# Retention followed by a routed feed-forward layer on one core: input loads, weight loads and two batches' feed-forward work moved between loop turns

## The chip, the cores and the metric

The kernel runs on one core of a Trainium2 chip. The metric is the device time of one execution in microseconds. Before the change three runs gave a median of 123.45 us (122.86 to 124.14). A core has five engines with a queue of instructions each: PE (matrix multiply; its weight loads are listed as PEld), DVE (VectorE), ACT (ScalarE), POOL (GpSimd) and SP, which here only issues transfers. Every engine works through its own queue in order and waits for others through semaphores. The transfers run on 16 DMA engines that SP's and POOL's issues share.

## The reference

Shapes: q, k, v are (4 batches, 8 heads, 768 positions, 64). The second layer has w_gate (512), w1 (512 x 1024), w2 (1024 x 512) and a capacity of 128.

```python
gamma = 1.0 - 2.0 ** (-5.0 - np.arange(H))
for t in range(S):                       # retention: a decaying state per head
    state = gamma * state + einsum('bhd,bhe->bhde', k[:, :, t], v[:, :, t])
    y[:, :, t] = scale * einsum('bhd,bhde->bhe', q[:, :, t], state)
x = y.transpose(0, 2, 1, 3).reshape(B, S, H * D)

scores = einsum('bsd,d->bs', x, w_gate)  # routing: 128 of 768 tokens of a batch
for b in range(B):
    top_idx = argpartition(-scores[b], capacity)[:capacity]
    xe = x[b, top_idx]
    ye = np.maximum(xe @ w1, 0.0) @ w2
    g = 1.0 / (1.0 + np.exp(-scores[b, top_idx]))
    out[b, top_idx] = x[b, top_idx] + g[:, None] * ye    # out is x elsewhere
```

## The kernel before, in words

The 768 positions of a batch are cut into three blocks of 256, so there are 12 blocks, numbered m = 0 to 11; block m belongs to batch b = m // 3 and is its block r = m % 3. The recurrence is written in chunks of 128: matmuls inside a chunk under a causal mask, and a state that is carried from chunk to chunk. All matmuls are bf16.

**The way of one block.**

- `load(m)` (L57) issues five transfers on SP: two halves of q, two of k, one of v, together 1.57 MB. The tiles lie in a pool of five buffers for each of q, k and v.
- `cast(m)` (L179) runs on POOL: qb is q times a decay table, kc is k in bf16, vb is v times a table. Four buffers of each.
- `transposes(m, "q")` and `(m, "k")` (L191) on PE, each copied out of PSUM by ACT as qT and kT. `turn_back(m)` (L201) transposes kT back to kb.
- `scores(m, part)` (L211): matmuls into pa, and a masking multiply on DVE into am.
- `inside(m)`, `across(m, u, py)` and `update(m, u)`: the outputs py of two chunks, and the state matmuls pst with their copies S on ACT.
- `finish(m, py)` (L270): ACT copies py to the output tile xo, DVE sums the routing scores from py (its product goes to a tile called junk). `put(m, xo)` (L284) issues two output stores on SP, 0.52 MB together.

**The way of one batch through the second layer.**

- `route_spread` and `route_beats` run once for each block: the scores are transposed to a row (pr) and compared (DVE, L315, L319, L322). `route_ranks` (PE, pk) and `route_index` (DVE, L354 and L357, idx) run once the three blocks of a batch are there.
- `route_fetch` (L360) is an indirect transfer on POOL's queue that gathers the 128 chosen rows from the output in memory into xg. It needs the batch's output stores to have landed, and the index.
- `route_gate` (product with w_gate: POOL for batches 0 to 2, DVE for batch 3), `route_turn` (PE transposes pg, copied by ACT as xT), `route_sigmoid` (ACT sums and takes exp, DVE adds one and takes the reciprocal).
- `ffn_up(b, 0)` and `(b, 1)` (matmuls ph, relu copy hT on ACT), `ffn_down` (matmuls pd), `ffn_add` (DVE, ye), `route_put` (indirect store on POOL's queue).

pr, pk, pg, ph, pd and the pb of `turn_back` take turns in one PSUM pool, psM, of two buffers, in the order of the program.

**The weights.** `load_weights(part)` (L159) is called for four parts: two halves of w1, two halves of w2. Each is a transfer on POOL's queue that reads 1.05 MB in f32 and writes 0.52 MB in bf16.

**The order.** The program is written in the order in which each engine is to work. Ahead of the loop stand `load(0)` to `load(3)` and the casts of blocks 0 and 1. The loop (L472) has 12 passes, here called turns. Turn m does, in this order: `load(m + 4)`; place -1; `cast(m + 2)`; in turns 1 to 4 one part of the weights; the q transposes of block m + 1; the second half of block m's scores; an update; place 0; the k transposes of block m + 1; place 1; `inside`, `across`, `finish`, an update, `put`; place 2; the first half of block m + 1's scores and `turn_back(m + 1)`; places 3 and 4. The routing and feed-forward steps are put into these places by a table (L441 to L458), entered as `at(turn, place, step)`; several steps at one place run in the order in which they were entered, which is by the last block of their batch. With m the last block of batch b (2, 5, 8, 11), the steps of a batch hang on the turn d of its fetch:

```python
            d = m + 3 if b < B - 2 else m + 2
            at(d, -1, route_fetch, b)
            at(d + 2, -1, route_gate, b)
            at(d + 2, 2, route_turn, b)
            at(d + 2, 4, route_sigmoid, b)
            at(d + 3, 0, ffn_up, b, 0)
            at(d + 3, 2, ffn_up, b, 1)
            at(d + 3, 3, ffn_down, b)
            at(d + 4, 1, ffn_add, b)
            at(d + 5, -1, route_put, b)
```

So d is 5, 8, 10, 13. What falls on turn 12 or later runs behind the loop, in the order of turns and places: the routing of batch 3 from its last block on, and all that is left of the feed-forward work.

Of the kernel before, what the change touches and what calls it, by code (L numbers as in the profile page):

```python
# [9 lines left out]
FT = mybir.dt.float32  # L10
BF = mybir.dt.bfloat16
# [7 lines left out]
def kernel(ctx: ExitStack, tc: tile.TileContext, q, k, v, w_gate, w1, w2, capacity, out):  # L19
    nc = tc.nc  # L20
    B, H, S, D = q.shape
    C = 128
# [3 lines left out]
    Dm = H * D  # L26
# [4 lines left out]
    NBLK = B * NM  # L31
# [11 lines left out]
    store = ctx.enter_context(tc.tile_pool(name="store", bufs=4))  # L43
    perb = ctx.enter_context(tc.tile_pool(name="perb", bufs=2))
# [12 lines left out]
    def load(m):  # L57
        b, r = divmod(m, NM)
        for nm, src in (("q", q), ("k", k), ("v", v)):
            ap = src[b, :, r * T:(r + 1) * T, :]  # L60
            if nm != "v":
                t = loads.tile([128, 2, 8, D], FT, name=nm + "f", tag=nm + "f")
                for half in range(2):
                    nc.sync.dma_start(t[:, half].rearrange("p j d -> p (j d)"),
                                      bass.AP(tensor=ap.tensor, offset=ap.offset + half * S * D,
                                              ap=[[8 * D, T // 8], [2 * S * D, HP], [1, 8 * D]]))
            else:
                t = loads.tile([128, H, 2, D], FT, name=nm + "f", tag=nm + "f")
                ap = bass.AP(tensor=ap.tensor, offset=ap.offset, ap=[[2 * D, 128], ap.ap[0], [1, 2 * D]])
                nc.sync.dma_start(t.rearrange("p h j d -> p h (j d)"), ap)  # L70
            raw[nm, m] = t
# [65 lines left out]

    load(2)
    load(3)
    before = consts.tile([128, C], FT)  # L140
    tokrow = consts.tile([128, S], FT)
    slotcol = consts.tile([128, 1], FT)
# [16 lines left out]
    def load_weights(part):  # L159
        if part < 2:  # L160
            n = DD // 2
            nc.gpsimd.dma_start(w1s[:, part * n:(part + 1) * n, :],
                                bass.AP(tensor=w1.tensor, offset=w1.offset + part * n * 128 * F,
                                        ap=[[F, 128], [128 * F, n], [1, F]]))
        else:
            n = FB // 2
            part -= 2
            nc.gpsimd.dma_start(w2s[:, part * n:(part + 1) * n, :],
                                bass.AP(tensor=w2.tensor, offset=w2.offset + part * n * 128 * Dm,
                                        ap=[[Dm, 128], [128 * Dm, n], [1, Dm]]))  # L170
# [8 lines left out]
    def cast(m):  # L179
        r = m % NM  # L180
        kc = nats.tile([128, 8, 2, D], BF, name="kc", tag="kc")
        vb = nats.tile([128, 2, H, D], BF, name="vb", tag="vb")
        qb = nats.tile([128, 8, 2, D], BF, name="qb", tag="qb")
        nc.gpsimd.tensor_mul(qb, raw["q", m].rearrange("p h j d -> p j h d"),  # L184
                             gq[:, r, :, :, None].to_broadcast([128, 8, 2, D]))
        nc.gpsimd.tensor_copy(kc, raw["k", m].rearrange("p h j d -> p j h d"))  # L186
        nc.gpsimd.tensor_mul(vb, raw["v", m].rearrange("p h j d -> p j h d"),  # L187
                             gv[:, 2 * r:2 * r + 2, :, None].to_broadcast([128, 2, H, D]))
        nat[m] = (kc, vb, qb)

    def transposes(m, nm):  # L191
        src = nat[m][2 if nm == "q" else 0]
        pt = psT.tile([128, 8, T // 8, HP], BF, name="pt", tag="pt")
        for i in range(8):
            nc.tensor.transpose(pt[:, i].rearrange("p s g -> p (s g)"), src[:, i], ident)  # L195
        t = work.tile([128, HP, T], BF, name=nm + "T", tag=nm + "T")
        nc.scalar.activation(t.rearrange("p g (s i) -> p g s i", i=8), pt.rearrange("p i s g -> p g s i"), AF.Copy)  # L197
        tr[nm, m] = t
# [12 lines left out]
    def scores(m, part):  # L211
        qT, kT = tr["q", m], tr["k", m]
        pa = psA.tile([128, 2, 2, 2, C], FT, name="pa", tag="pa")
        for d in range(2):
            dd = 2 * part + d
            for j in range(2):
                for u in range(2):
                    for half in range(2):
                        r = slice(half * 64, half * 64 + 64)
                        nc.tensor.matmul(pa[u * 64:u * 64 + 64, half, d, j, :], kT[r, dd, u * C:(u + 1) * C].rearrange("p (s j) -> p s j", j=2)[:, :, j],  # L220
                                         qT[r, dd, u * C:(u + 1) * C], start=True, stop=True)
        am = work.tile([128, 2, 2, 2, C], BF, name="am", tag=f"am{part}")
        nc.vector.tensor_mul(am.rearrange("p a b c d -> p (a b) (c d)"), pa.rearrange("p a b c d -> p (a b) (c d)"),  # L223
                             causal.rearrange("p a b -> p (a b)")[:, None, :].to_broadcast([128, 4, 2 * C]))
        att[m, part] = am
# [3 lines left out]
    def inside(m):  # L229
        vb = nat[m][1]  # L230
        py = [psY.tile([C, H, D], FT, name=f"py{u}", tag=f"py{u}") for u in range(2)]
        for h in range(H):
            dd, half = divmod(h, 2)
            for j in range(2):
                for u in range(2):
                    r = slice(u * 64, u * 64 + 64)
                    nc.tensor.matmul(py[u][:, h, :], att[m, dd // 2][r, half, dd % 2, j, :], vb[r, j, h, :],  # L237
                                     start=(h == 0 and j == 0), stop=True, skip_group_check=True)
        return py
# [30 lines left out]
    def finish(m, py):  # L270
        b, r = divmod(m, NM)
        if r == 0:
            batch[b] = {"sc": perb.tile([128, NC], FT, name="sc", tag="sc")}
        xo = store.tile([C, 2, Dm], FT, name="xo", tag="xo")

        for u in range(2):
            nc.scalar.activation(xo[:, u, :], py[u].opt(), AF.Copy)  # L277
            w = 1 - u
            junk = store.tile([C, Dm], BF, name="junk", tag="junk")
            nc.vector.scalar_tensor_tensor(junk, py[w].opt(), 1.0, wgB, OP.mult, OP.mult,  # L280
                                           accum_out=batch[b]["sc"][:, 2 * r + w:2 * r + w + 1])
        return xo
# [76 lines left out]

    def route_fetch(b):  # L360
        st = batch[b]
        xg = perb.tile([128, Dm], FT, name="xg", tag="xg")
        nc.gpsimd.indirect_dma_start(  # L363
            out=xg, out_offset=None, in_=flat[:(b + 1) * S], in_offset=bass.IndirectOffsetOnAxis(ap=st["idx"][:, 0:1], axis=0),
            bounds_check=(b + 1) * S - 1, oob_is_err=True)
        st["xg"] = xg
# [71 lines left out]
    def at(t, place, f, *args):  # L438
        slots.setdefault((t, place), []).append((f, args))

    for m in range(NBLK):  # L441
        b, r = divmod(m, NM)
        at(m + 1, 0, route_spread, b, r)
        at(m + 1, 1, route_beats, b, r)
        if r == NM - 1:
            at(m + 1, 3, route_ranks, b)
            at(m + 1, 4, route_index, b)

            d = m + 3 if b < B - 2 else m + 2
            at(d, -1, route_fetch, b)  # L450
            at(d + 2, -1, route_gate, b)
            at(d + 2, 2, route_turn, b)
            at(d + 2, 4, route_sigmoid, b)
            at(d + 3, 0, ffn_up, b, 0)
            at(d + 3, 2, ffn_up, b, 1)
            at(d + 3, 3, ffn_down, b)
            at(d + 4, 1, ffn_add, b)
            at(d + 5, -1, route_put, b)  # L458

    def slot_work(t, place):  # L460
        for f, args in slots.pop((t, place), ()):
            f(*args)
# [7 lines left out]
    turn_back(0)  # L470

    for m in range(NBLK):  # L472
        if m + 4 < NBLK:
            load(m + 4)
        slot_work(m, -1)
        if m + 2 < NBLK:
            cast(m + 2)
        if 1 <= m < 5:
            load_weights(m - 1)
        if m + 1 < NBLK:  # L480
            transposes(m + 1, "q")
        scores(m, 1)
        update(m, 0)
        slot_work(m, 0)
        if m + 1 < NBLK:
            transposes(m + 1, "k")
        slot_work(m, 1)
        py = inside(m)
        for u in range(2):
            across(m, u, py)  # L490
        xo = finish(m, py)
        update(m, 1)
        put(m, xo)
        slot_work(m, 2)
        if m + 1 < NBLK:
            scores(m + 1, 0)
            turn_back(m + 1)
        slot_work(m, 3)
        slot_work(m, 4)
# [37 lines left out]
```

## Time and profile before

| | us |
|---|---|
| median of three runs | 123.45 (122.86 to 124.14) |
| the profiled execution | 123.08 |
| its span in the trace | 121.4 |
| PE busy | 83.1 (68%) |
| DVE busy | 75.0 (62%) |
| ACT busy | 76.8 (63%) |
| POOL busy | 77.2 (64%) |

Transfers: 29.88 MB, mean 246 GB/s over the span; 25.43 MB of them on SP's queue, 4.20 MB on POOL's (counted by what is written). No engine is busy over the whole span, so the page is read by stretches of time. On the timelines a line gives the start, the duration, the engine, the source line, the operation with its output and inputs, and, in brackets, how long the engine had stood idle before it and what ended that. All times count from the start of the span. PE's pipelined matmuls are merged into one line for a group.

### The profile page before, as it was taken

What the parts mean: (1) busy time and instruction counts of PE and PEld (TensorE: products, weight loads), DVE (VectorE), ACT (ScalarE), POOL (GpSimd) and SP (SyncE); (2) the same over time, 40 slices, a digit from 0 to 9 for tenths busy, and PEclk for the clock granted to TensorE, in tenths of its full rate; (3) what the DMA queues carried; (4) which work ended last, traced back from release to release, by engine and by line L of the source; (5) the groups of instructions that cost most, each with busy time, mean ns of one, the idle gap of its engine ahead of it and who ended that gap; (6) DMA issues with size and microseconds to landing.
All of it is one profiled execution on the core that took longest, in us unless ns stands there. A gap on an engine that the chain in (4) does not pass through costs nothing. (4 is left out here: it accounts for less than half of the span.)

```text
span 121.4 us, 4113 instructions
## 1 busy us (share of the span) xinstructions
PE 83.1 (68%) x1701; PEld 64.9 (53%) x1708; DVE 75.0 (62%) x217; ACT 76.8 (63%) x141; POOL 77.2 (64%) x72
## 2 busy tenths in 40 slices
PE   0046798968676896609959879796497785694920
PEld 0034576856664685408847768474495663371700
DVE  6001347689899788913987849489759394924120
ACT  6233587999976699905578999593489942431500
POOL 6658999999998290899659999799034000231230
PEclk9999999999999999965799999999769999999998
DMA  2999999999999999999999999985215113203202
GB/s 58 299 299 343 337 343 364 345 346 391 296 280 275 344 279 290 370 365 283 327 389 360 387 359 392 354 297 192 92 24 195 48 57 115 86 5 86 86 0 86
DMA packets 25250, 29.88 MB, mean 246 GB/s; under 512 B 1552, under 2 KB 14864, under 8 KB 25232
## 3 DMA queue, kind: packets, MB, share of 16 engines
q1 hardware_dynamic: 22992, 25.43, 62.6%
q0 software_dynamic: 2240, 4.20, 14.7%
q8 instruction: 13, 0.21, 0.7%
q14 instruction: 5, 0.04, 0.1%
HBM read 24.38 MB, written 7.34 MB: 261 GB/s over the span
## 5 line engine op out<-in xcount | busy, mean ns | idle before, releaser
L223 DVE TENSOR_TENSOR am<-pa,causal 128x1024 bf16<-128x1024 f32 x24 | 29.3, 1222 | 21.2 <-PE pa L220 21.1
L187 POOL TENSOR_TENSOR vb<-vf,gv 128x1024 bf16<-128x1024 f32 x12 | 22.8, 1900 | 6.1 <-DMA vf<-in_v_dram 6.1
L184 POOL TENSOR_TENSOR qb<-qf,gq 128x1024 bf16<-128x1024 f32 x12 | 22.8, 1904 | 4.9 <-DMA qf<-in_q_dram 4.8
L197 ACT ACTIVATE qT<-pt 128x1024 bf16<-128x1024 bf16 x12 | 12.3, 1022 | 14.3 <-PE pt L195 14.3
L277 ACT ACTIVATE xo<-py 128x512 f32<-128x512 f32 x24 | 14.4, 600 | 8.0 <-DVE junk L280 6.5
L195 PE MATMUL pt<-ident,qb 128*128 128x128 bf16 x96 | 9.5, 257 | 12.0 <-POOL qb L184 12.0
L280 DVE SCALAR_TENSOR_TENSOR junk<-py,wgB 128x512 bf16<-128x512 f32 x24 | 15.6, 689 | 1.8 <-PE py L247 1.8
L268 ACT ACTIVATE S<-pst 64x256 bf16<-64x256 f32 x40 | 14.9, 373 | 1.0 <-PE pst L263 0.4
L220 PE MATMUL pa<-qT,kT 64*64 64x128 bf16 x384 | 11.7, 243 | 5.6 <-DVE am L223 4.0
L431 POOL DMA_INDIRECT out_dram<-ye,idx x4 | 4.2, 1040 | 16.9 <-DVE ye L426 13.6
L195 PEld LDWEIGHTS <-qb 128*128 128x128 bf16 x96 | 7.4, 116 | 13.0 <-POOL qb L184 12.7
L197 ACT ACTIVATE kT<-pt 128x1024 bf16<-128x1024 bf16 x12 | 12.3, 1021 | 2.1 <-PE pt L195 2.1
L186 POOL CAST kc<-kf 128x1024 bf16<-128x1024 f32 x12 | 12.4, 1036 | 1.6 <-DMA kf<-in_k_dram 1.6
L208 ACT ACTIVATE kb<-pb 128x1024 bf16<-128x1024 bf16 x12 | 12.3, 1022 | 1.8 <-PE pb L206 1.7
L220 PEld LDWEIGHTS <-kT 64*64 64x64 bf16 x384 | 7.9, 118 | 8.1 <-issue 4.6
L263 PE MATMUL pst<-vb,kb 64*64 64x64 bf16 x320 | 9.5, 203 | 1.6 <-ACT kb L208 1.6
L195 PE MATMUL pt<-ident,kc 128*128 128x128 bf16 x96 | 8.8, 244 | 2.0 <-ACT qT L197 1.6
L341 PE MATMUL pk<-beats,ones 128*128 128x512 bf16 (+3 forms) x29 | 5.8, 304 | 6.0 <-ACT kb L208 4.5
L237 PE MATMUL py<-vb,am 64*128 64x64 bf16 x384 | 9.0, 198 | 1.0 <-issue 0.6
L195 PEld LDWEIGHTS <-kc 128*128 128x128 bf16 x96 | 7.6, 111 | 3.6 <-issue 2.5
L263 PEld LDWEIGHTS <-kb 64*64 64x64 bf16 x320 | 7.8, 118 | 3.2 <-ACT kb L208 2.3
L363 POOL DMA_INDIRECT xg<-out_dram,idx x4 | 4.3, 1084 | 8.1 <-PE pa L220 3.8
(79 smaller groups left out, 147.6 us busy)
## 6 DMA issues: line engine op xcount, KB each, us to landing
qf<-in_q_dram SPq DMA_DIRECT2D x24, 256.0 KB, 6.5
kf<-in_k_dram SPq DMA_DIRECT2D x24, 256.0 KB, 7.1
vf<-in_v_dram SPq DMA_DIRECT2D x12, 512.0 KB, 9.7
out_dram<-xo SPq DMA_DIRECT2D x24, 256.0 KB, 6.1
w1s<-in_moe_w_dram POOLq DMA_DIRECT2D x2, 512.0 KB, 8.6
w2s<-in_moe_w_dram POOLq DMA_DIRECT2D x2, 512.0 KB, 10.3
wgB<-in_moe_w_gate_dram SPq DMA_DIRECT2D x1, 256.0 KB
xg<-out_dram,idx POOLq DMA_INDIRECT x4, 5.2
```

The lines of the kernel that those rows point to most:

```text
L184: nc.gpsimd.tensor_mul(qb, raw["q", m].rearrange("p h j d -> p j h d"), gq[:, r, :, :, None].to_broadcast([128, 8, 2, D]))
L186: nc.gpsimd.tensor_copy(kc, raw["k", m].rearrange("p h j d -> p j h d"))
L187: nc.gpsimd.tensor_mul(vb, raw["v", m].rearrange("p h j d -> p j h d"), gv[:, 2 * r:2 * r + 2, :, None].to_broadcast([128, 2, H, D]))
L195: nc.tensor.transpose(pt[:, i].rearrange("p s g -> p (s g)"), src[:, i], ident)
L197: nc.scalar.activation(t.rearrange("p g (s i) -> p g s i", i=8), pt.rearrange("p i s g -> p g s i"), AF.Copy)
L208: nc.scalar.activation(kb.rearrange("p j h d -> p (j h d)"), pb.rearrange("p j g x -> p (j g x)"), AF.Copy)
L220: nc.tensor.matmul(pa[u * 64:u * 64 + 64, half, d, j, :], kT[r, dd, u * C:(u + 1) * C].rearrange("p (s j) -> p s j", j=2)[:, :, j], qT[r, ...
L223: nc.vector.tensor_mul(am.rearrange("p a b c d -> p (a b) (c d)"), pa.rearrange("p a b c d -> p (a b) (c d)"), causal.rearrange("p a b -> ...
L263: nc.tensor.matmul(pstate[b][half * 64:half * 64 + 64, dd, :], kb[r, j, h, :], vb[r, j, h, :], start=(c == 0 and dd == 0 and j == 0), stop ...
L268: nc.scalar.activation(t[r, :, half * 64:half * 64 + 64], pstate[b][r], AF.Copy)
L277: nc.scalar.activation(xo[:, u, :], py[u].opt(), AF.Copy)
L280: nc.vector.scalar_tensor_tensor(junk, py[w].opt(), 1.0, wgB, OP.mult, OP.mult, accum_out=batch[b]["sc"][:, 2 * r + w:2 * r + w + 1])
```

## The change

`load(4)` joins the loads ahead of the loop, and turn m issues `load(m + 5)` instead of `load(m + 4)`; the pool of five buffers is as it was. The four weight parts are issued in turns 2, 4, 6 and 7 instead of 1, 2, 3 and 4. The fetches of batches 0 and 1 go one turn later (d is 6, 9, 10, 13), and all that hangs on them with them. `ffn_down` goes from place 3 to place 4 for every batch. The output tile xo has six buffers instead of four, junk two instead of four, the gathered tile xg three instead of two.

With these turns the table meets itself in two turns: batch 0's up and down matmuls fall on turn 9, where batch 2's ranks are made; batch 1's fall on turn 12, behind the loop, beside the routing of batch 3. Batch 1's sigmoid falls on turn 11, place 4, so that its gate steps on DVE stand ahead of the last beats, where before batch 1's add stood.

```diff
@@ -137,6 +137,7 @@
     load(2)
     load(3)
+    load(4)
@@ -271,12 +272,12 @@
-        xo = store.tile([C, 2, Dm], FT, name="xo", tag="xo")
+        xo = store.tile([C, 2, Dm], FT, name="xo", tag="xo", bufs=6)
...
-            junk = store.tile([C, Dm], BF, name="junk", tag="junk")
+            junk = store.tile([C, Dm], BF, name="junk", tag="junk", bufs=2)
@@ -359,7 +360,7 @@
-        xg = perb.tile([128, Dm], FT, name="xg", tag="xg")
+        xg = perb.tile([128, Dm], FT, name="xg", tag="xg", bufs=3)
@@ -446,14 +447,14 @@
-            d = m + 3 if b < B - 2 else m + 2
+            d = m + (4, 4, 2, 2)[b]
...
-            at(d + 3, 3, ffn_down, b)
+            at(d + 3, 4, ffn_down, b)
@@ -470,13 +471,13 @@
-        if m + 4 < NBLK:
-            load(m + 4)
+        if m + 5 < NBLK:
+            load(m + 5)
         slot_work(m, -1)
         if m + 2 < NBLK:
             cast(m + 2)
-        if 1 <= m < 5:
-            load_weights(m - 1)
+        if m in (2, 4, 6, 7):
+            load_weights((2, 4, 6, 7).index(m))
```

## The prediction

> **What bounds the kernel now.** I read the 40 slices first, then sums over stretches, then the timelines of POOL, PE, ScalarE and DVE where a stretch looked odd. Slices of 3.03 us:
>
> ```profile
> POOL 6658999999998290899659999799034000231230
> PEclk9999999999999999965799999999769999999998
> DMA  2999999999999999999999999985215113203202
> ```
>
> Transfers run without a gap until about 80 us, then hardly at all. PEclk dips twice, in slices 17-19 (52-61 us) and 28-29 (85-91 us). The stretches (PE, PEld, DVE, ACT, POOL busy, clock, DMA share, GB/s) say which engine starves:
>
> ```profile
> 30.00:40.00 10.00, 6.58 (x163) 5.25 (x163) 9.29 (x26) 7.83 (x13) 9.49 (x8) 1.00 1.11 288
> 40.00:50.00 10.00, 8.47 (x240) 6.86 (x237) 8.47 (x23) 8.96 (x16) 4.37 (x4) 1.00 1.11 316
> 50.00:60.00 10.00, 5.82 (x134) 4.93 (x126) 5.52 (x17) 4.94 (x8) 9.16 (x7) 0.66 1.12 328
> ```
>
> From 40 to 50 POOL, the first station of every block, works only 4.37 of 10 us; from 50 to 60 PE, DVE and ACT starve. POOL's timeline tells why:
>
> ```profile
> 42.73 1.89 POOL L184 TENSOR_TENSOR qb<-qf,gq 128x1024 bf16<-128x1024 f32 x1 [2.51 <-DMA qf<-in_q_dram]
> 48.74 1.90 POOL L187 TENSOR_TENSOR vb<-vf,gv 128x1024 bf16<-128x1024 f32 x1 [3.13 <-DMA vf<-in_v_dram]
> 50.58 0.80 POOL L168 DMA_DIRECT2D w2s<-in_moe_w_dram  x1
> 52.84 1.91 POOL L184 TENSOR_TENSOR qb<-qf,gq 128x1024 bf16<-128x1024 f32 x1
> ```
>
> Block 6's q and v come late, so block 7's qb starts at 52.84, and PE pays:
>
> ```profile
> 50.01 0.62 PE L206 MATMUL pb<-ident,kT 128*128 128x128 bf16 x8
> 54.80 1.03 PE L195 MATMUL pt<-ident,qb 128*128 128x128 bf16 x8 [4.18 <-POOL qb L184]
> ```
>
> This is the only wait of PE for POOL after turn 1. The ends of turns (start of the second xo copy, ScalarE) make it visible: turns 3 to 11 end at 37.47, 44.40, 50.30, 60.71, 67.64, 75.37, 84.14, 92.24, 99.68; their lengths from turn 4 on are 6.93, 5.90, **10.41**, 6.93, 7.73, 8.77, 8.10, 7.44; turn 3 took 6.49. From there on engines hand work to each other, and after 100.25 (end of the last score sum) only the routing of batch 3 counts:
>
> ```profile
> 101.69 0.38 PE L304 MATMUL pr<-identf,sc 128*128 128x128 f32 x2
> 102.56 0.74 DVE L315 TENSOR_SCALAR_CACHE_REDUCE beats<-row,sc 128x512 bf16<-128x512 f32 x1
> 106.66 0.21 DVE L357 TENSOR_SCALAR idx<-acc 128x1 int32<-128x1 f32 x1
> 111.26 0.63 PE L373 MATMUL pg<-identf,xg 128*128 128x128 f32 x4 [1.32 <-DMA xg<-out_dram,idx]
> ```
>
> PE and DVE stand behind batch 1's down matmul and its add here (101.69, 102.56); the index is ready 6.6 us after the last score.
>
> **Loads and weights.** The SP queue moved 25.43 MB in 62.6% of 121.4 us, 335 GB/s: a block (1.57 MB) costs 4.7 us, a pair of output stores (0.52 MB) 1.6, a weight part (512 KB on the page are its bf16 result, so 1.05 MB read) 3.1. In 30-40, with three parts under way, the counted rate fell from 358 to 288, so parts do take their share. Up to block 6's v (48.7) before, parts 0, 1 and most of 2 had to land (issued 27.73, 33.39, 39.42, landing 8.4 to 10.3 us later); after, only part 0, so it comes some 6 us sooner, at 43, and POOL, contiguous from 28 us, needs it at 41 to 43. Block 7's q landed at 50.1 (issued 41.3, 8.8 to landing); two parts (6.2) and one pair of stores (1.6) less put it at 42 to 44. So qb 7 ends at about 46 where PE asks at 50.6: **the stall goes with 4 to 5 us to spare.** Turn 6 then takes 6.49 like turn 3: -3.9. Next late would be qb 8: it stands behind vb 7 and the first fetch, which waits for turn 2's stores; those leave behind load 7, landing 49 to 51.5. Fetch (1.1) and qb (1.9) end by 54.5; PE asks at 59.4 (turn 6's new end 56.8, and 2.6 for the ranks as from 60.71 to 63.34). No stall.
>
> The load ahead is worth less than it says: SP's stores waited 9.5 us, six times, for loads of v to land, so few transfers fly at once, and an earlier issue only swaps places with a store. That is the 1.6 above.
>
> Parts 2 and 3 now compete with blocks 9 to 11. Block 10's q landed at 71.1 (POOL's last wait before 71.17); a store pair less and about half of part 3 less gives 68 to 69.5. POOL then has vb 9, part 3's issue (0.80) and batch 0's product (1.27) in front: qb 10 ends at 71.5. With the turns below turn 8 ends at 50.30+6.49+6.93+5.90 = 69.6, and PE asks 0.85 later (as 68.49 after 67.64), at 70.5, so **+1.0** in turn 9. Bounds: 0, and 3.7 if qb 10 ends at 74.2 as before. Block 11's qb (79.6 before) isn't asked for before 80.
>
> **Clock.** Turn 10's stretch from pt to py took 90.21-86.99 = 3.22 us, the same in turn 7 65.60-63.34 = 2.26: the dip cost 0.96, after a PE pause of 1.85 us. I put nothing on the 1.0 stall and 0.96 into the bound. The Trainium skill, "TensorE: Matmul & The Clock Gate", Part 1, has the clock halve after an idle window of about 3.4 us. By it a 1.0 us pause costs nothing; turn 6's 4.18 agrees, turn 10's 1.85 does not, so the row goes into the bound.
>
> **Routing moved in the loop.** Prices from pairs of turns with equal r: gather transposes, sigmoid and up matmuls, turn 8 against 5, 7.73-5.90 = 1.83 (of it 1.94 us of DVE waiting for the sigmoid's exp, partly beside other work); down matmul and add, turn 9 against 3, 8.77-6.49 = 2.28. After: turn 7 6.93; turn 8 5.90 (-1.83); turn 9 6.49+1.83 = 8.32 (-0.45); turn 10 6.93+2.28 = 9.21 (+1.11; the down matmul's 1.9 now stands behind batch 2's ranks, ahead of block 11's transposes, and the first pk buffer is free by then); turn 11 has neither sigmoid nor up matmuls of batch 1: 7.44-1.83 = 5.61 (-1.83). Sum with turn 6: -6.9; with the stall **-5.9**. Fetches move from POOL's turn 5 and 8 to 6 and 9, same 1.1 each; put 0 moves into turn 11, when POOL has no casts left.
>
> **The end.** Batch 1's transposes, sigmoid and all its matmuls now meet batch 3's routing. From the last score (0.0): ScalarE copies xo and xT to 0.6, sums prod to 1.25, exp 1.5; DVE's two gate steps to 1.95 stand ahead of the beats: L315 to 3.45, L319 and L322 to 4.4, wonb 4.65. That is 0.1 sooner than before, since the add and the down matmul left. But batch 2's pg shares pr's PSUM buffer (two in rotation), so it runs at 4.45 to 5.1, and both pk follow it: to 7.0; batch 2's exp and gate on DVE end at 7.1, ahead of the two L354 (to 8.25); index 8.6 instead of 6.6, +2.0. Behind that PE does batch 1's down matmul (1.9), waits for ye (0.85), batch 2's up and down to 13.4; xg lands at 8.6+0.9+3.4 = 12.9. So pg of batch 3 starts at 13.4, not 11.0: **+2.4**. Bounds: -2.3 if the freed places alone tell (beats at 100.25 instead of 102.56), and +8.3 if everything moved (up 2.1, relu 1.2, pg and xT 1.3, prod and exp 1.2, down 1.9, ye 0.75) adds up in a row.
>
> Six output tiles, two junk, three gathered tiles: ScalarE never waited for a store, so nothing; the third gathered tile spares fetch 2 (turn 10) a wait for batch 0's add.
>
> **Sum.** -5.9+2.4 = -3.5 on an execution of 123.08 (span 121.4 and 1.7 around it): 119.6; that execution lies 0.37 under the median, so I forecast **119.9**.
>
> **Rivals.**
> Late loads: parts 2 and 3 hold block 10 as long as before, qb 10 at 74.2: stall 3.7 and cold 0.96, and gap and end otherwise as above: -6.9+4.7+2.4 = +0.2, 123.6. For it: loads take 6 to 7 us to land even at the end; against: 1.6 us of stores leave its way. 16%.
> The end (slower): moved work on the path. It decides once the end grows by more than the 5.9 won; at the full +8.3 it gives +2.4, 125.8. For it: two tiles of PSUM serve three batches; against: DVE and ScalarE idle over half of 100-110 (4.97, 3.37 busy). 20%.
> The load ahead does nothing, as SP allows no more in flight: block 7's q loses 1.6 of 4 to 5 us to spare, the time stays 119.9; it is within the forecast.
>
> **Chances and range.** The three runs spread by 1%, so within 1.2 us is no change. Forecast 60%, all of it faster. Late loads split 2 faster, 11 same, 3 slower; the end 3 same, 17 slower; 4% of others slower. Faster 0.62, same 0.14, slower 0.24. Low: no stall and an end of +0.6, -6.3: 117.2. High: into the end's case, with 13% above: 125.0.
>
> **What would show it.** Right: no PE wait of 4 us near 50; turn 6 at 6.5; POOL waits gone in 40-50; index 8 to 9 us after the last score. Wrong: POOL waiting for q or v of blocks 8 to 10 with PE behind it; turn 9 over 10; part landings beyond 12; batch 3's pg waiting for pd instead of xg by more than 2 us.

## The result and the profile after

| | before | changed |
|---|---|---|
| median of the runs, us | 123.56 (122.86 to 124.14, 4 runs) | 120.55 (119.63 to 122.26, 4 runs) |
| the profiled execution | 123.08 | 119.63 |
| its span | 121.4 | 117.9 |
| turns 6 to 11, from end to end of turn | 49.4 | 42.6 |
| last score sum to the end of the span | 21.1 | 24.5 |

The ratio is 0.9685, with a 95% interval from 0.9598 to 0.9772: faster. Ratios leave out disturbed runs (over 1.5% above the fastest of their kernel), medians do not. Forecast were a median of 119.9, measured 120.55, and -3.5 us for the profiled execution; that one fell by 3.45. In a later set, beside its own runs of the kernel before, the changed kernel won less: 121.06 against 123.22, a ratio of 0.983 (last set of the experiments).

The slices of the changed kernel, 2.95 us each:

```profile
POOL 6376999999999989837999841995309100213330
PEclk9999999999999999999999999999999967999996
DMA  2899999999999999999999999999254220022012
```

Transfers still run without a gap to about 83 us: the same bytes. POOL has no hole at 40 to 50 us, and the first clock dip (a stretch with PE's granted clock at half, below also called cold) is gone. The one that is left while PE works lies in slices 32 and 33, 94 to 100 us, at the end of the kernel. The stretches (PE, PEld, DVE, ACT, POOL busy, clock, DMA share, GB/s) say the same in microseconds:

```profile
30.00:40.00 10.00, 6.64 (x163) 5.29 (x163) 9.25 (x25) 7.80 (x13) 9.98 (x7) 1.00 1.12 327
40.00:50.00 10.00, 8.37 (x241) 6.84 (x239) 8.51 (x23) 9.00 (x16) 9.12 (x8) 1.00 1.09 345
50.00:60.00 10.00, 6.93 (x163) 5.62 (x163) 8.99 (x25) 7.10 (x12) 7.28 (x6) 1.00 1.09 356
```

POOL works 9.12 instead of 4.37 us from 40 to 50, and DVE 8.99 instead of 5.52 from 50 to 60. On POOL's timeline block 6's v and block 7's qb:

```profile
41.69 1.90 POOL L188 TENSOR_TENSOR vb<-vf,gv 128x1024 bf16<-128x1024 f32 x1 [0.41 <-PE pr L305]
44.35 1.92 POOL L185 TENSOR_TENSOR qb<-qf,gq 128x1024 bf16<-128x1024 f32 x1
```

vb of block 6 starts at 41.69 (48.74 before), qb of block 7 ends at 46.27. PE's next q transposes follow the kb transposes at once and at full clock:

```profile
49.97 0.62 PE L207 MATMUL pb<-ident,kT 128*128 128x128 bf16 x8
50.43 0.61 PE L196 MATMUL pt<-ident,qb 128*128 128x128 bf16 x8
```

Turns 3 to 11 end at 37.42, 44.35, 50.27, 56.74, 63.67, 69.59, 76.96, 87.10, 92.84. Turns 6 to 11 take 6.47, 6.93, 5.92, 7.37, 10.14, 5.74. In turn 10 PE waits for ACT:

```profile
78.90 1.13 PE L342 MATMUL pk<-beats,ones 128*128 128x128 bf16 x6 [1.72 <-ACT hT L415]
```

The end got longer; the last score sum ends at 93.43, and then, on PE and DVE:

```profile
94.87 0.38 PE L305 MATMUL pr<-identf,sc 128*128 128x128 f32 x2
95.07 0.73 DVE L316 TENSOR_SCALAR_CACHE_REDUCE beats<-row,sc 128x512 bf16<-128x512 f32 x1
101.45 0.21 DVE L358 TENSOR_SCALAR idx<-acc 128x1 int32<-128x1 f32 x1
106.42 0.60 PE L374 MATMUL pg<-identf,xg 128*128 128x128 f32 x4
111.41 0.75 DVE L427 SCALAR_TENSOR_TENSOR ye<-pd,gt,xg 128x512 f32<-128x512 f32 x1 [2.82 <-PE pd L421]
```

The index comes 8.2 us after the last score sum (6.6 before), batch 3's pg 13.0 (11.0 before). That explains 2.0 of the 3.4 us, and up to 0.5 of that may be the clock dip: in a second profile of the changed kernel ("changed, again" below), whose dip lay earlier, the index came 7.8 and pg 12.5 us after the last score sum. The rest stands on POOL's queue, in the indirect transfers at the end, first of the kernel before, with its last sum on DVE:

```profile
107.73 1.04 POOL L363 DMA_INDIRECT xg<-out_dram,idx  x1 [3.76 <-PE ph L412]
111.93 1.03 POOL L431 DMA_INDIRECT out_dram<-ye,idx  x1 [3.17 <-DVE prod L384]
116.29 0.75 DVE L426 SCALAR_TENSOR_TENSOR ye<-pd,gt,xg 128x512 f32<-128x512 f32 x1 [3.29 <-remote]
117.32 1.01 POOL L431 DMA_INDIRECT out_dram<-ye,idx  x1 [4.35 <-DVE ye L426]
```

and of the changed one:

```profile
102.55 1.07 POOL L364 DMA_INDIRECT xg<-out_dram,idx  x1 [10.61 <-DVE idx L358]
106.78 1.04 POOL L432 DMA_INDIRECT out_dram<-ye,idx  x1 [3.17 <-issue]
110.38 1.00 POOL L432 DMA_INDIRECT out_dram<-ye,idx  x1 [2.56 <-DMA out_dram<-ye,idx]
113.88 0.99 POOL L432 DMA_INDIRECT out_dram<-ye,idx  x1 [2.50 <-issue]
```

Three stores now follow fetch 3, not two. Each starts only when the transfer before it has landed: 106.78, 110.38, 113.88, steps of 3.6 and 3.5 us. The program gives each a slice of the output that begins at its first row (L432), so that the slices overlap; that this is why they wait is argued from the program, not tested. Batch 3's sum ye ended at 112.16, so its store, the last work of the kernel, started 1.72 us late; before, it started 0.28 us after ye (117.32 against 117.04).

### The profile page after: what moved, and what is told of

Its sections match the earlier page's. It is cut to its first block, busy times and chain, and to the rows that moved or that the text cites. A ratio compares the mean times of both kernels' runs of the same rounds, so it can differ in the third digit from the quotient of the medians.

```text
span 117.9 us, 4118 instructions
## 1 busy us (share of the span) xinstructions
PE 81.1 (69%) x1708; PEld 63.7 (54%) x1708; DVE 74.9 (64%) x217; ACT 76.8 (65%) x141; POOL 77.3 (66%) x72
## 5 line engine op out<-in xcount | busy, mean ns | idle before, releaser
L198 ACT ACTIVATE qT<-pt 128x1024 bf16<-128x1024 bf16 x12 | 12.3, 1022 | 10.8 <-PE pt L196 10.8
L221 PE MATMUL pa<-qT,kT 64*64 64x128 bf16 x384 | 11.1, 232 | 8.6 <-DVE am L224 7.0
L196 PE MATMUL pt<-ident,qb 128*128 128x128 bf16 x96 | 8.2, 235 | 8.1 <-POOL qb L185 8.1
L432 POOL DMA_INDIRECT out_dram<-ye,idx x4 | 4.1, 1018 | 11.4 <-issue 5.7
L196 PEld LDWEIGHTS <-qb 128*128 128x128 bf16 x96 | 6.4, 105 | 9.0 <-POOL qb L185 8.6
L413 PE MATMUL ph<-xT,w1s 128*128 128x128 bf16 x128 | 9.1, 231 | 3.1 <-ACT xT L376 2.7
L413 PEld LDWEIGHTS <-w1s 128*128 128x128 bf16 x128 | 8.2, 104 | 4.0 <-issue 2.5
L415 ACT ACTIVATE hT<-ph 128x512 bf16<-128x512 f32 x8 | 4.8, 597 | 7.5 <-PE ph L413 7.4
L196 PE MATMUL pt<-ident,kc 128*128 128x128 bf16 x96 | 8.1, 233 | 2.2 <-ACT qT L198 1.6
```

Source lines behind the costliest of these rows:

```text
L413: nc.tensor.matmul(ph[:, j, :], w1s[:, dd, ff * 128:(ff + 1) * 128], st["xT"][:, dd, :], start=(j == 0 and dd == 0), stop=True, skip_group ...
```

## The experiments

The twelve runs went to three chips, four kernels at a time; each set has its own runs of the kernel before. "Sum" is turns 6 to 11 and "end" the time from the last score sum to the end of the span, both of the profiled execution (49.4 and 21.1 before).

| kernel | median us (runs) | before, same chip | ratio | sum | end |
|---|---|---|---|---|---|
| loads and weights only | 126.44 (123.26 to 127.54) | 122.66 | none given | 52.7 | 21.1 |
| routing only | 124.26 (123.44 to 125.21) | 122.66 | 1.018 (1.008 to 1.029) | 47.0 | 24.4 |
| no store of batch 1 | 120.57 (119.98 to 120.99) | 122.66 | 0.986 (0.977 to 0.994) | 45.0 | 23.3 |
| batch 1 as before | 127.03 (126.21 to 129.31) | 122.66 | 1.035 (1.025 to 1.046) | 52.2 | 21.2 |
| four ahead | 122.31 (121.74 to 124.09) | 122.70 | 1.000 (0.990 to 1.011) | 45.2 | 24.5 |
| early weights | 122.69 (121.97 to 123.60) | 122.70 | 1.005 (0.995 to 1.016) | 45.4 | 24.3 |
| late weights only | 126.04 (123.30 to 127.33) | 122.70 | none given | 49.2 | 21.2 |
| batch 1 sooner after its fetch | 120.65 (119.44 to 122.41) | 122.70 | 0.980 (0.967 to 0.993) | 45.1 | 22.9 |
| changed, again | 121.06 (119.52 to 122.23) | 123.22 | 0.983 (0.973 to 0.992) | 43.7 | 24.1 |
| four ahead, again | 121.56 (120.88 to 125.07) | 123.22 | 0.988 (0.981 to 0.994) | 44.3 | 24.1 |
| batch 1 sooner, again | 119.88 (118.54 to 121.30) | 123.22 | 0.973 (0.964 to 0.982) | 45.4 | 21.1 |
| four ahead, batch 1 as before | 120.01 (118.08 to 121.94) | 123.22 | 0.966 (0.956 to 0.977) | 46.0 | 21.2 |

**Loads and weights only.** Against the changed kernel:

```diff
-            d = m + (4, 4, 2, 2)[b]
+            d = m + 3 if b < B - 2 else m + 2
-            at(d + 3, 4, ffn_down, b)
+            at(d + 3, 3, ffn_down, b)
```

> Loads five ahead, weights in turns 2, 4, 6, 7 and the buffer counts of the change; fetches, ffn_down and all that hangs on them at the turns of before. Theory (the stall of turn 6 is 3.9 us of the gain, and the new end is paid for by the moved routing): no wait of PE for POOL near 50 us, turn 6 at 6.5 us, turns 7 to 11 as before (6.9, 7.7, 8.8, 8.1, 7.4, sum 39.0), 21.1 us from the last score sum to the end of the span: span 117.5, time 119.3. Rival (the late weight parts take the gain back in the loop): w2 or block 10 is late, PE waits 2 us or more in turns 8 to 10, span 119.5 or more. Rival (the routing's move is what pays): span 120 or more.

It came out the other way: 126.44 us, the lowest run 123.26 against 119.3 expected, and turn 6 took 9.84. POOL's timeline shows the fetches of batches 0 and 1 in turns 5 and 8:

```profile
52.32 1.13 POOL L364 DMA_INDIRECT xg<-out_dram,idx  x1 [5.02 <-DMA qf<-in_q_dram]
76.23 1.09 POOL L364 DMA_INDIRECT xg<-out_dram,idx  x1 [5.79 <-DMA kf<-in_k_dram]
```

POOL reached them sooner than before, and then stood 5.0 and 5.8 us for the output stores that they need, with the casts queued behind. (The wait is for several semaphores, and the profile names a load. That the stores are what the fetch waits for follows from the program; their landing is shown below, under "Four kernels side by side", for a fetch that waits in the same way.) This profiled execution ran at a low mean clock, 0.923, so its turns are read for the waits alone.

**Routing only.** Against the changed kernel:

```diff
-    load(4)
-        if m + 5 < NBLK:
-            load(m + 5)
+        if m + 4 < NBLK:
+            load(m + 4)
-        if m in (2, 4, 6, 7):
-            load_weights((2, 4, 6, 7).index(m))
+        if 1 <= m < 5:
+            load_weights(m - 1)
```

> Fetches, ffn_down and buffers as in the change; loads four ahead and weights in turns 1 to 4 as before. Theory: the stall in turn 6 stays, less the first fetch that stood ahead of block 7's qb (1.4 us): PE waits 2.8 us, turn 6 takes 9.0; turns 7 to 11 take 36.1 us together as in the changed kernel (39.0 before); 24.4 us from the last score sum to the end (21.1 before). Against before -1.4-2.9+3.3 = -1.0: span 120.4, time 122.1. Rival (the routing's move is what pays): span 118.5 or less, time 120.2 or less.

124.26 us, 2 us over the theory; its rival, that the routing's move pays by itself, falls. PE's timeline has the expected stall in turn 6 and a second one in turn 8:

```profile
52.98 0.62 PE L195 MATMUL pt<-ident,qb 128*128 128x128 bf16 x8 [2.61 <-POOL qb L184]
67.32 0.62 PE L195 MATMUL pt<-ident,qb 128*128 128x128 bf16 x8 [1.75 <-POOL qb L184]
```

The end is 24.4, as in the changed kernel. **So neither half of the change is faster than the kernel before; only both together are.**

**No store of batch 1.** Batch 1's indirect store is left out, so its 128 rows keep the first layer's values.

```diff
-            at(d + 5, -1, route_put, b)
+            if b != 1:
+                at(d + 5, -1, route_put, b)
```

> The changed kernel without the indirect store of batch 1, so its 128 rows keep the first layer's values. Theory (in the changed kernel the three last indirect stores follow each other, each waiting until the one before has landed, the first until fetch 3 has landed): the store of batch 2 is issued right after its add, that of batch 3 within 0.4 us of its add instead of 1.7: 1.4 us less from the last score sum to the end (23.0 instead of 24.4), span 116.5, time 118.2. Rival (the end is set by PE's and DVE's chain alone, the stores wait beside it): no change, 24.4 and 119.6.

The last sum on DVE, and the two stores that are left on POOL:

```profile
114.14 0.75 DVE L427 SCALAR_TENSOR_TENSOR ye<-pd,gt,xg 128x512 f32<-128x512 f32 x1 [2.82 <-PE pd L421]
```

```profile
110.37 1.23 POOL L432 DMA_INDIRECT out_dram<-ye,idx  x1 [4.04 <-DVE ye L427]
115.17 1.00 POOL L432 DMA_INDIRECT out_dram<-ye,idx  x1 [3.56 <-DVE ye L427]
```

The last store starts 0.28 us after its sum (115.17 against 114.89) instead of 1.72, and the end is 23.3, 1.2 less, though pg came 0.2 later here. The row of stores is shown as the cause of that part. The time didn't fall to 118.2, since this execution's turns 9 to 11 took 8.2, 10.8 and 6.5 us at a mean clock of 0.936 (the changed kernel's: 7.4, 10.1, 5.7 at 0.977).

**Batch 1 as before.**

```diff
-            d = m + (4, 4, 2, 2)[b]
+            d = m + (4, 3, 2, 2)[b]
```

> The changed kernel with batch 1's fetch back in turn 8 (d is 6, 8, 10, 13), so its up and down matmuls are done in turn 11 and its store is issued ahead of fetch 3. Theory: turns 6 to 10 as in the changed kernel, turn 11 at 7.5 us instead of 5.7, index 6.6 to 7 us after the last score sum, 21.1 to 21.6 us from there to the end: span 116.4, time 118.1. Rival (what leaves the end comes back in full in turns 10 and 11): span 117.9, time 119.6.

Turn 11 at 7.50 and the end at 21.2 are as the theory had it. Turn 9 is not: 15.23 us. Fetch 1 on POOL, and PE behind it:

```profile
75.96 1.13 POOL L364 DMA_INDIRECT xg<-out_dram,idx  x1 [9.78 <-DMA kf<-in_k_dram]
```

```profile
79.09 1.03 PE L196 MATMUL pt<-ident,qb 128*128 128x128 bf16 x8 [7.71 <-POOL qb L185]
```

One number of the table of turns held POOL for 9.78 us and PE for 7.71. The theory had left out what fetch 1 waits for.

**Four ahead, early weights, late weights only, batch 1 sooner after its fetch.** These four take the parts apart. The first undoes the load ahead, the second the weights' turns, both against the changed kernel, as in the diff of "routing only". The third is the kernel before with only the weights' turns changed. The fourth leaves fetch 1 in turn 9 and does all that follows it a turn sooner:

```diff
             at(d, -1, route_fetch, b)
+            d -= b == 1
             at(d + 2, -1, route_gate, b)
```

> The changed kernel with loads four ahead again; late weights and moved routing stay. Theory (the load ahead only swaps places with a pair of stores, 1.6 us of transfer): in the changed kernel block 10's qb ended at 68.2 and PE asked at 69.9, blocks 7 to 9 had more to spare, so nothing is lost: PE waits for POOL 0 to 1 us after turn 1, turns 6 to 11 sum to 42.6 to 43.6, span 117.9 to 119. Rival (the load ahead is needed): PE waits for POOL 1.5 us or more in turns 6 to 9, sum 44 or more, span 119.5 or more.

> The changed kernel with the weights in turns 1 to 4 again; loads five ahead and moved routing stay. Theory: the routing-only kernel waited 2.6 us for block 7's qb and 1.75 for block 9's; a store pair (1.6) less in front leaves 1.0 and 0.2: turns 6 to 11 sum to 43.6 to 44, span 119.0 to 119.5. Rival (the weights' turns are all of the gain): PE waits 2.5 us or more, span 120.5 or more. Rival (they are nothing): no wait, span 117.9.

> The kernel before with nothing but the weights moved to turns 2, 4, 6, 7. Theory (with five loads ahead, fetches at their old turns hold POOL, because the stores they wait for are issued behind one more load; with four ahead those stores come 5 us sooner): POOL waits 1 to 3 us for fetch 0 and up to 4 for fetch 1, against 5.0 and 5.8 with five ahead; PE waits 0 to 1 us, turns 6 to 11 sum to 45.4 to 46.5, end 21.1: span 117.4 to 118.5, time 119.3 to 120.4. Rival (fetches at the old turns hold POOL whatever the loads do, once POOL runs sooner): PE waits 3 us or more, span 121 or more.

> The changed kernel, with batch 1's fetch left in turn 9, but all that follows it one turn sooner (product in turn 10, matmuls in turn 11, its store ahead of fetch 3). Theory (in the kernel with batch 1 as before, only the place of the fetch on POOL did harm, 9.8 us in front of block 10): no such wait, turns 6 to 10 as in the changed kernel, turn 11 at 7.5, end 21.1 to 21.6: turns 6 to 11 sum to 44.3, span 116.0 to 116.6, time 117.7 to 118.3. Rival (batch 1's work in the loop costs more than it saves at the end): span 117.9 or more.

*Four ahead*: PE waited for POOL 0.28 us after turn 1, as the theory had it, yet the time was 122.31, no better than the kernel before on that chip. The longer turns 10 and 11 (11.7 and 6.4 us) came with clock dips, so the question stayed open for a run beside the changed kernel.

*Early weights*: PE's timeline shows what the weights are worth with all else changed, 1.11 and 0.95 us of waiting (the theory had 1.0 and 0.2):

```profile
51.81 0.62 PE L196 MATMUL pt<-ident,qb 128*128 128x128 bf16 x8 [1.11 <-POOL qb L185]
60.83 0.62 PE L196 MATMUL pt<-ident,qb 128*128 128x128 bf16 x8 [0.95 <-POOL qb L185]
```

The sum is 45.4, over the theory's 43.6 to 44; the second wait was in turn 7, where none was expected, and the clock dipped behind it, so that turn 7 took 9.20 us instead of 6.93. Turn 6 took 6.70, so most of its stall is gone without late weights too: the wait for block 7's qb is 4.18 us before, 2.61 with the routing alone, 1.11 with five loads ahead as well.

*Late weights only*: turn 6 fell to 6.48, so the weights alone remove the stall of turn 6. The time was 126.04 all the same, the lowest run 123.30, where 119.3 to 120.4 were expected. The two fetches at their old turns hold POOL no longer:

```profile
45.82 1.13 POOL L363 DMA_INDIRECT xg<-out_dram,idx  x1 [0.31 <-issue]
67.43 1.10 POOL L363 DMA_INDIRECT xg<-out_dram,idx  x1 [0.30 <-issue]
```

0.31 and 0.30 us, where five loads ahead made 5.0 and 5.8 of it. But PE met another wait in turn 8, in batch 0's down matmul:

```profile
77.26 1.86 PE L420 MATMUL pd<-w2s,hT 128*128 128x512 bf16 x4 [2.31 <-DMA w2s<-in_moe_w_dram]
```

The last weight part, issued at 66.3, isn't there when turn 8 needs it. PE's next transposes run cold (1.06 us for 8 instead of 0.61), and turn 9 takes 12.71. So the late weights need batch 0's matmuls a turn later.

*Batch 1 sooner after its fetch*: 120.65; turns 8 to 10 as expected, but with dips in turns 4, 6, 11 and the end. It was run again with the others.

**Four kernels side by side, with more rounds.** Loads four or five ahead, batch 1 late or soon:

> The changed kernel itself, beside three others on one chip. Theory: turns 6 to 11 sum to 42.6, more only where the clock dips, 24.4 from the last score sum to the end; time 119.6 to 121. Rival (its first measurement was a lucky clock): 122 or more, like the four-ahead kernel.

> The changed kernel with loads four ahead, again. In its first run PE waited for POOL 0.3 us after turn 1, and the longer turns 10 and 11 (11.7, 6.4 instead of 10.1, 5.7) came with a clock dip. Theory (the load ahead is worth nothing): within 0.6 us of the changed kernel on the same chip. Rival (it is worth the 2 us by which its time was higher on another chip): 1.5 us or more above it.

> The changed kernel with all of batch 1 behind its fetch one turn sooner, again. Theory: turn 11 at 7.5 instead of 5.7, end 21.2 instead of 24.4: 1.5 us below the changed kernel on the same chip, 118.1 to 119.5. Rival (the moved work costs in the loop and in the clock what it saves): within 0.6 us of it.

> Loads four ahead, late weights, batch 0 a turn late as in the change, batch 1 at its turns of before (fetch in turn 8). With five ahead that fetch held POOL 9.8 us. Theory (it is the load ahead that puts the stores late): POOL waits under 1 us for fetch 1, turn 9 at 7.4 instead of 15.2, turn 11 at 7.5, end 21.2; 1.5 us below the four-ahead kernel, 118 to 120. Rival (the fetch waits whatever the loads do): turn 9 at 10 or more, 123 or more.

Medians: late batch 1, five ahead 121.06, four ahead 121.56; soon, five ahead 119.88, four ahead 120.01. By the medians five loads ahead make -0.5 and -0.1 us against four, by the ratios -0.6 with batch 1 late and +0.8 with it soon: less than these runs can tell. Batch 1 sooner makes -1.2 and -1.5 by the medians, -1.2 and -2.6 by the ratios, where the theory had -1.5. Fetch 1 at its old turn 8 with four ahead, from the last kernel's POOL timeline:

```profile
67.20 1.14 POOL L363 DMA_INDIRECT xg<-out_dram,idx  x1 [0.17 <-issue]
```

0.17 us instead of 9.78, and turn 9 at 7.37 instead of 15.23. The two kernels differ in the load ahead alone. SP's issues say why, here the stores of block 5, which fetch 1 needs, first with four ahead, then with five:

```profile
57.44 0.96 SPq L287 DMA_DIRECT2D out_dram<-xo  x2
62.14 3.70 SPq L288 DMA_DIRECT2D out_dram<-xo  x2
```

With four they landed 6.1 us after their issue, at 63.5 and 64.2, before POOL came to the fetch (67.0). With five they stand behind the load of block 10; they landed 11.6 and 9.6 us after their issue, the second at 75.1, and the fetch began at 75.96. In the kernel with batch 1 sooner the last store starts at 113.19, 0.27 us after its sum:

```profile
113.19 1.00 POOL L432 DMA_INDIRECT out_dram<-ye,idx  x1 [4.39 <-DVE ye L427]
```

Both versions with batch 1 soon lie under the changed kernel in their medians, by 1%; their intervals overlap with its own, so "beats the kernel before" is shown, "beats the changed kernel" only likely.

## Why the prediction was right, and where it was off

- *The stall of turn 6 goes, -3.9.* Right: -3.94 (10.41 to 6.47). qb 7 ended at 46.27 (forecast about 46) with PE asking at 50.43. The weights' turns are enough for it, shown by "late weights only" with turn 6 at 6.48. They are not the only way: with early weights the other two parts take 3.07 of the 4.18 us of waiting away, 1.57 by the routing (the first fetch no longer stands ahead of qb 7) and 1.50 by the load ahead, close to the 1.6 that the prediction had for a pair of stores. With late weights the kernels with four loads ahead show no wait of PE for POOL in turn 6 either, so that the load ahead has nothing left to win there.
- *A stall of 1.0 in turn 9.* It didn't come. Block 10's q landed at 66.3 and not at 68 to 69.5, qb 10 ended at 68.2, PE asked at 69.9. Why the loads came 2 us sooner than byte counting gave was not tried.
- *Turns 7 to 11.* Forecast 6.93, 5.90, 8.32, 9.21, 5.61; measured 6.93, 5.92, 7.37, 10.14, 5.74. Turns 9 and 10 are off by -0.95 and +0.93; that they cancel is luck. Why turn 9 is shorter was not tried. In turn 10 the first pk now takes the buffer of batch 0's second up matmuls, whose relu copy stands on ACT behind the output copies, and PE waited 1.72 us for it. The prediction had looked at the buffer behind pk, not at the one ahead.
- *The end, +2.4.* The mechanism was right: batch 1's gate steps ahead of the beats, pg 2 (batch 2's) behind them, and PE busy until 106.4, 0.4 us after the gathered rows had landed; index 8.2 (forecast 8.6), pg 13.0 (forecast 13.4). The term was too small by the row of three stores, 1.4 us, less the 0.4 that pg came sooner than forecast: +3.4. Its step "xg lands, then pg" followed PE and DVE to the end and not POOL's queue. The Trainium skill, "DMA: Bandwidth & Descriptors", section "Anatomy of one DMA — SWDGE (gpsimd) path", puts a transfer of this path at about 2.0 us plus its bytes over 436 GB/s: an estimate of 2.6 us for 256 KB. Here a store of the row landed 2.7 to 2.8 us after its issue began, close to that; the next began 0.8 us later still, so that the row goes in steps of 3.5.
- *Fetches move, same 1.1 each.* The number was right and the reason to move them was missed. With five loads ahead the stores come behind one more load, and a fetch at its old turn holds POOL 5 to 10 us. Likewise the late weights need batch 0's matmuls a turn later (2.31 us and a cold PE otherwise). The prediction priced the parts as if each stood alone; "loads and weights only" at 126.4 and "routing only" at 124.3 show that they don't. The sum held since all the parts were there.
- *Sums.* The terms of the full bound of the end add up to 8.45, not 8.3, and 119.6 and 0.37 make 119.97, not 119.9; neither changes a conclusion.
- *Not tried by themselves:* the new place of `ffn_down` and the counts of buffers.
- *The rivals.* Late loads: fallen, no wait of PE for POOL after turn 1. The end: it grew by 3.4, less than the 6.8 won. The load ahead does nothing: open. It is worth 1.5 us of waiting where the weights are early; with late weights the four kernels side by side have it at -0.6 and +0.8 us, and their intervals are wider than that.

Two terms missed and offset each other: the loop gave 6.8 instead of 5.9, the end took 3.4 instead of 2.4. That the sum came out within 0.1 us on the profiled execution is luck to that extent.

## What to carry to other kernels

Where transfers are the bound, put off first what is needed last, and then ask what each queue will meet sooner: a fetch on a compute engine's queue that waits for stores holds all the work behind it, and an extra load ahead delays those stores. A change of several parts is priced as a whole, for each part can be the cover of another. At the end of a kernel, follow every queue to its last instruction: indirect transfers that must see each other land cost 3.5 us apiece in a row here.

## What the runs showed of the hardware

One and the same kernel on one chip, the changed one, took between 119.52 us (mean clock 0.980) and 122.23 (0.945) in six runs. That is as much as the whole effect of some parts here, and it is why the waits of a trace told these kernels apart better than their times did. The dips move as well: the two profiles of this kernel, from two sets of runs, have theirs in slices 32 and 33 and in slices 30 and 31.

No long pause was needed for a dip. The kernel before had its second one behind a pause of PE of only 1.85 us: the granted clock was at half from 86.5 us on, and in the 3.41 us ahead of that PE was busy for 1.25. Its first dip began at 52.3, when the pause of 4.18 us had lasted 1.7; in the 3.41 us ahead of it PE was busy for 1.47. The prediction took that pause as agreeing with an idle window of about 3.4 us; these rows don't bear that out.
